# Key-side softmax reciprocals moved from VectorE to ScalarE as exp(-ln), with row normalisations of tiles 2 and 3 freed and a new instruction order

## The chip, the cores and the metric

The kernel runs on one core of a Trainium2 chip. The metric is device microseconds of one execution, lower is better. Kernels are compared only within the same rounds. A difference under 2% counts as the same. All runs used here are fast; the granted TensorE clock of the profiled ones is 1.0 (0.999 in one), that of the timed ones 0.994 to 1.0.

## The reference

```python
x = A_x                                   # 2048 rows x 640
h  = x + A_ref(layernorm(x), wqkv, w_phi, wo)
h2 = h + B_ref(layernorm(h), w_gate, w_up, w_down)

# A_ref: 32 heads of 20 columns
pk    = einsum("bhsd,hdf->bhsf", k, w_phi)                 # pq likewise from q
phi_k = concat([softmax(pk), softmax(-pk)], axis=-1)       # over 20 columns
kv, z = einsum("bhsf,bhsd->bhfd", phi_k, v), sum_s(phi_k)
o     = einsum(phi_q, kv) / (einsum(phi_q, z) + 1e-6)      # then @ wo
# B_ref: ((x @ w_gate) * (x @ w_up)) @ w_down
```

The change touches one step: the two softmaxes of the key side. Per row there are 2 x 32 sums of 20 exponentials each, and the exponentials are multiplied by the reciprocals of the 64 sums.

## The kernel before

The rows are worked in 16 tiles of 128. Each operation has a name and a key; a list scheduler places the operations of every engine in the order of a table of keys, and semaphores follow from the data. So **a table of keys is an order of instructions for TensorE (PE), VectorE, ScalarE, the Pool engine and the queue of transfers (SP)**.

The key side of a tile `t` (bodies cut):

```python
for s in range(2):                                  # exp(+pk), exp(-pk) out of PSUM
    G.op("act",  "Kx%d_%d" % (t, s), ... func=AF.Exp, scale=1.0 - 2.0 * s ...)
G.op("dve",  "Ks%d" % t, ... tensor_reduce(out=SR[.., 0, :], in_=ek, op=ALU.add) ...)
G.op("dve",  "Kr%d" % t, ... reciprocal(out=SR[.., 1, :], in_=SR[.., 0, :]) ...)
G.op("pool", "Kn%d" % t, ... tensor_tensor(out=ek, in0=ek, in1=SR[.., 1, :], op=ALU.mult) ...)
# then KV<t>: the key-value matmuls on PE
```

The rows of a tile are normalised (`xn`), and transposed (`xt`) before the projections. The transposes of tiles 0 to 3 are matmuls on PE. Those of tiles 4 to 15 are transfers in the one SP queue, which also carries later rows of the input, the transposes of the query weights (`wqt0` to `wqt4`), later the transposes of the attention output (`oT`) and the down-projection weights (`wd0` to `wd3`):

```python
TPE = (0, 1, 2, 3)
...
G.op("dve", "xn%d" % t, xn, 0.5, LD, [...], [xb], 10 * t - 22,
     alts=[] if t in TPE else [("act", act_c(640, True), LA)])   # may go to ScalarE
...
else:                                                            # t not in TPE
    G.op("sp", "xt%d" % t, ... dma_start_transpose(out=xnT[tile t], in_=xn) ...)
```

PSUM has 8 banks; three hold the key-value accumulators during the key stage, and a projection needs a pair of what is left.

The softmax here doesn't subtract the row's maximum and nothing guards it: scores larger than these inputs give would overflow.

Of the kernel before, what the change touches and what calls it, by code (L numbers as in the profile page):

```python
# [8 lines left out]
AF = mybir.ActivationFunctionType  # L9
# [30 lines left out]
TPE = (0, 1, 2, 3)  # L40
# [7 lines left out]
x0:0.7 wk0:1.18:1 wk2:1.66:1 wk4:2.14 x1:0.7 wv0:2.14 wv2:2.62:1 wv4:3.1:1 x2:1.66:1 x4:2.62:1 x6:3.58 w5:1.18 x8:4.06 x10:21.175 x12:23.385 x14:19.475  # L48
wqt0:26.485 wqt1:25.265 wqt2:37.415 wqt3:38.635 wqt4:32.535 wo0:51.896 wo2:53.336 wg0:52.856 wu0:51.416 wg1:54.296 wu1:50.936 wg2:49.976 wu2:53.816
wg3:49.016 wu3:52.376 wg4:49.496 wu4:50.456 id0:4.17 gl0:1.52 eps:1.77 id1:4.72 gla0:2.19 glb0:2.63 gla4:2.41 glb4:3.07 gla1:1.97 glb1:3.73 gla2:3.29  # L50
glb2:3.95 gla3:2.85 glb3:3.51 va1:0.7 glx:4.47 kv1:5.12 zero:0.7 warm0:1.08 warm1:1.51 warm2:1.94 warm3:2.37 warm4:2.8 warm5:3.23 warm6:3.66 warm7:4.09
warm8:4.52 warm9:4.74 Ph0:5.42 Ph1:5.2:1 Ph2:5.432:1 WT0:5.27 WTe0:5.819 WT1:5.549 WTe1:6.443:1 WT2:7.062 WTe2:7.612:1 WT3:7.342 WTe3:8.03 WT4:10.677
WTe4:11.226 F1_0:6.747 Fe1_0:7.332:1 F1_1:7.9 Fe1_1:8.485 F1_2:8.215 Fe1_2:9.108:1 F1_3:8.628 Fe1_3:9.732 F1_4:12.143 Fe1_4:12.728:1 L1s0:3.847
L1a0:4.847 L1s1:3.027 L1a1:4.667 L1s2:9.687 L1a2:10.687 L1s3:8.867 L1a3:10.507 L1s4:10.797 L1a4:12.937 L1s5:11.617 L1a5:15.297 L1s6:13.547 L1a6:15.187
L1s7:14.367 L1a7:15.407 L1s8:16.755 L1a8:18.075 L1s9:15.935 L1a9:25.745 L1s10:25.855 L1a10:27.495 L1s11:26.675 L1a11:28.425 L1s12:27.605 L1a12:37.695
L1s13:32.295 L1a13:37.805 L1s14:34.995 L1a14:37.915 L1s15:38.025 L1a15:40.057 L1l0:5.177 L1e0:5.607 L1l1:4.957 L1e1:5.397 L1l2:10.977 L1e2:11.849
L1l4:15.845 L1e4:16.688 L1n4:16.998 L1n5:17.398 L1n6:17.198 L1n7:17.598 L1l8:28.715 L1e8:29.558 L1n8:30.068 L1n9:29.868 L1n10:30.468 L1n11:30.268
L1l12:40.347 L1e12:40.777 L1n12:42.793 L1n13:42.593 L1n14:42.993 L1n15:43.193 xn0:6.288 xt0:7.621 xte0:8.448:1 xn1:5.788 xt1:6.468 xte1:7.018:1
xn2:12.437 xt2:13.833 xte2:14.598 xn3:13.047 xt3:14.112 xte3:15.517:1 xn4:18.035:1 xt4:19.955 xn5:21.241:1 xt5:22.165 xn6:17.575 xt6:18.255 xn7:23.365
xt7:24.045 xn8:31.105:1 xt8:33.755 xn9:30.392:1 xt9:31.315 xn10:33.065:1 xt10:34.975 xn11:35.025:1 xt11:36.195 xn12:43.213:1 xt12:44.136 xn13:44.72  # L60
xt13:46.576 xn14:43.926:1 xt14:45.356 xn15:44.22 xt15:47.796 V0_0:10.133 V0_1:10.405 V0_2:11.871 V0_3:13.001 V0_4:13.273 Ve0:13.975 K0_0:14.391
K0_1:14.663 K0_2:14.935 K0_3:15.206 K0_4:15.478 Kx0_0:16.065 Kx0_1:17.411 Ks0:19.605 Kr0:21.485 Kn0:24.024 KV0:27.975 V1_0:9.59 V1_1:9.862 V1_2:11.6
V1_3:12.458 V1_4:12.73 Ve1:13.351 K1_0:9.047 K1_1:9.318 K1_2:10.956 K1_3:11.227 K1_4:13.561 Kx1_0:15.221 Kx1_1:16.788 Ks1:18.185 Kr1:21.025 Kn1:21.665
KV1:28.651 V2:19.825 Ve2:21.955 K2:15.75 Kx2_0:18.748 Kx2_1:19.995 Ks2:21.945 Kr2:23.865 Kn2:26.383 KV2:32.043 V3:17.108 Ve3:19.371 K3:18.466
Kx3_0:20.618 Kx3_1:22.578 Ks3:24.325 Kr3:29.955 Kn3:30.668 KV3:34.078 V4:23.9 Ve4:25.626 K4:25.258 Kx4_0:26.886 Kx4_1:27.72 Ks4:30.875 Kr4:33.115
Kn4:35.386 KV4:38.829 V5:32.719 Ve5:34.402 K5:26.616 Kx5_0:28.935 Kx5_1:29.768 Ks5:33.575 Kr5:37.235 Kn5:37.875 KV5:42.221 V6:21.183 Ve6:23.201
K6:22.541 Kx6_0:24.17 Kx6_1:25.003 Ks6:28.535 Kr6:30.415 Kn6:33.027 KV6:42.897 V7:29.327 Ve7:31.818 K7:30.685 Kx7_0:32.442 Kx7_1:33.778 Ks7:35.815
Kr7:38.845 Kn7:40.234 KV7:45.247 V8:37.47 Ve8:39.305:1 K8:39.505 Kx8_0:41.133 Kx8_1:41.966 Ks8:42.8 Kr8:45.22 Kn8:45.86 KV8:48.639 V9:34.754 Ve9:36.382
K9:36.112 Kx9_0:37.74 Kx9_1:38.574 Ks9:40.167 Kr9:41.767 Kn9:43.393 KV9:50.674 V10:40.863 Ve10:42.59 K10:43.888 Kx10_0:45.517 Kx10_1:46.35 Ks10:47.183
Kr10:48.783 Kn10:49.423 KV10:54.066 V11:56.101 Ve11:57.73 K11:45.923 Kx11_0:47.551 Kx11_1:48.384 Ks11:49.243 Kr11:52.094 Kn11:52.734 KV11:60.491  # L70
V12:57.46 Ve12:59.088:1 K12:47.281 Kx12_0:49.008 Kx12_1:49.841 Ks12:50.674 Kr12:52.554 Kn12:55.093 KV12:61.167 V13:54.742 Ve13:56.371 K13:51.35
Kx13_0:52.978 Kx13_1:53.811 Ks13:55.243 Kr13:56.843 Kn13:59.811 KV13:62.473 V14:58.818 Ve14:60.446 K14:49.315 Kx14_0:50.944 Kx14_1:51.777 Ks14:53.014
Kr14:54.614 Kn14:57.452 KV14:63.149 V15:64.14 Ve15:65.769 K15:52.708 Kx15_0:54.435 Kx15_1:55.268 Ks15:57.602 Kr15:59.84 Kn15:62.17 KV15:68.736
KVe0:70.902 KVe1:69.682 KVe2:70.292 F0_0:61.843 Fe0_0:62.428 F0_1:60.176 Fe0_1:61.07 F0_2:63.825 Fe0_2:64.41:1 F0_3:43.573 Fe0_3:44.64 F0_4:62.158
Fe0_4:62.743:1 Q0_0:67.657 Qx0_0_0:69.006 Qx0_0_1:69.523 Q0_1:70.491 Qx0_1_0:72.357 Qx0_1_1:71.84 Q0_2:69.412 Qx0_2_0:70.761 Qx0_2_1:71.278 Q0_3:65.499
Qx0_3_0:66.848 Qx0_3_1:67.364 Q0_4:66.578 Qx0_4_0:67.927 Qx0_4_1:68.444 Q1_0:82.274 Qx1_0_0:83.623 Qx1_0_1:84.14 Q1_1:74.419 Qx1_1_0:76.285
Qx1_1_1:75.768 Q1_2:83.353 Qx1_2_0:85.219 Qx1_2_1:84.702 Q1_3:78.691 Qx1_3_0:80.04 Qx1_3_1:80.557 Q1_4:79.77 Qx1_4_0:81.636 Qx1_4_1:81.12 Q2_0:72.995
Qx2_0_0:74.344 Qx2_0_1:74.86 Q2_1:91.421 Qx2_1_0:93.287 Qx2_1_1:92.77 Q2_2:75.498 Qx2_2_0:76.847 Qx2_2_1:77.364 Q2_3:85.79 Qx2_3_0:87.14 Qx2_3_1:87.656
Q2_4:93.859 Qx2_4_0:95.208 Qx2_4_1:95.725 Q3_0:90.342 Qx3_0_0:92.208 Qx3_0_1:91.691 Q3_1:88.228 Qx3_1_0:89.577 Qx3_1_1:90.094 Q3_2:71.57 Qx3_2_0:72.92
Qx3_2_1:73.436 Q3_3:76.577 Qx3_3_0:77.926 Qx3_3_1:78.443 Q3_4:80.85 Qx3_4_0:82.715 Qx3_4_1:82.199 wd0:95.208 wd1:95.688 wd2:99.088 wd3:98.608  # L80
N0_1:72.65 N0_0:74.074 sr0:73.265 rho0:74.689 A0:75.059 B0:76.089 dd0:77.119 rd0:77.509 o0:77.989 oT0:79.41 O0:84.432 h0:86.123 L2s0:87.175 L2a0:88.175
L2v0:88.626 L2r0:89.25 hc0:88.465 hT0:89.996 N1_1:77.656 N1_0:78.346 sr1:78.271 rho1:78.961 A1:79.331 B1:80.361 dd1:81.391 rd1:81.781 o1:82.261:1
oT1:83.173 O1:86.87 h1:88.498 L2s1:89.43 L2a1:90.56 L2v1:90.85 L2r1:92.28 hc1:90.93:1 hT1:91.61 N2_1:89.307 N2_0:89.652 sr2:90.25 rho2:90.74 A2:91.43
B2:92.46 dd2:93.49 rd2:93.88 o2:94.36 oT2:96.168 O2:107.58 h2:109.249 L2s2:110.352 L2a2:111.524 L2v2:111.814 L2r2:112.164 hc2:111.814 hT2:112.737
N3_1:81.929 N3_0:78.001 sr3:82.993 rho3:83.483 A3:83.853 B3:84.883 dd3:85.913 rd3:86.875 o3:87.355 oT3:88.776 O3:92.5 h3:94.18 L2s3:95.111 L2a3:96.241
L2v3:96.531 L2r3:99.163 hc3:96.611:1 hT3:97.388 N4_1:94.938 N4_0:89.997 sr4:95.931 rho4:96.421 A4:97.111 B4:98.313 dd4:99.343 rd4:99.733 o4:100.213
oT4:101.634 O4:111.121 h4:112.75 L2s4:113.811 L2a4:114.821 L2v4:115.111 L2r4:115.851 hc4:115.111 hT4:116.035 N5_1:104.505 N5_0:104.16 sr5:105.295
rho5:105.785 A5:106.155 B5:107.185 dd5:108.387 rd5:108.949 o5:109.429 oT5:110.85 O5:116.775 h5:118.403 L2s5:119.335 L2a5:120.335 L2v5:120.625
L2r5:121.125 hc5:120.625:1 hT5:121.305 N6_1:99.995 N6_0:98.558 sr6:100.61 rho6:101.271 A6:101.641 B6:102.843 dd6:104.045 rd6:104.435 o6:104.915
oT6:106.336 O6:121.393 h6:123.021 L2s6:124.083 L2a6:125.093 L2v6:125.383 L2r6:128.155 hc6:126.805:1 hT6:127.485 N7_1:140.642 N7_0:142.066 sr7:141.257  # L90
rho7:142.681 A7:143.051 B7:144.081 dd7:145.55 rd7:145.94 o7:146.42 oT7:147.841 O7:153.093 h7:154.844 L2s7:155.895 L2a7:157.025 L2v7:157.346
L2r7:158.425 hc7:157.315 hT7:158.716 N8_1:112.48 N8_0:112.825 sr8:113.501 rho8:114.631 A8:115.001 B8:116.031 dd8:117.633 rd8:118.023 o8:118.503
oT8:119.924 O8:123.096 h8:125.203 L2s8:128.285 L2a8:129.315 L2v8:129.605 L2r8:130.295 hc8:129.795:1 hT8:130.475 N9_1:149.165 N9_0:149.51 sr9:149.78
# [113 lines left out]
def act_c(n, ptr=False):  # L207
    return (0.18 if ptr else 0.09) + n / 1200.0
# [10 lines left out]
LD, LA, LP, LT = 0.18, 0.21, 0.15, 0.27  # L219
# [3 lines left out]
def build_graph():  # L223
    G = Graph()
    T = {}
# [255 lines left out]
    for t in range(NT):  # L481
        kk = 10 * t
# [546 lines left out]
```

## Time and profile before

| | before |
|---|---|
| median of 3 runs | 283.46 us (283.19 to 283.81) |
| span of the profiled execution | 280.6 us (that execution timed 282.35 us) |
| PE busy | 275.4 us, 98% |
| waits of PE in all | 2.0 us |
| first transposes that need the second key weights | 7.87 us |
| last matmul ends, span less that | 278.2 us, 2.4 us |

The span is the time between the first and the last record on the core; the timed figure is some 1.75 us longer. The prediction below shows the busy shares, the chain, the waits and the head.

A view that the prediction did not show, and that became the important one, is the SP queue before, from 20 to 28 us (columns: start, length of the issues, engine, line, operation, out<-in, count). The transfers are named by what they move: `xnT<-xn` are transposes of normalised tiles, `scratch<-in_A_wqkv_dram` transposes of query weights, and further below `x_all` input rows.

```profile
22.53 1.20 SPq L458 DMA_TRANSPOSE xnT<-xn  x1
...
25.64 2.66 SPq L300 DMA_TRANSPOSE scratch<-in_A_wqkv_dram  x2
```

The transpose at 22.53 is that of tile 5; a load of rows and the transpose of tile 7 follow, and only then, at 25.64, two query weight transposes. Tile 5 landed at 26.45 us. PE wanted it at 27.35: the unbroken 13.58 us of matmuls from 15.13 that the prediction shows end at 28.71, and the last ten of them (1.36 us) are tile 5's key projection. So it had 0.9 us to spare.

### The profile page before, as it was taken

What the parts mean: (1) busy time and instruction counts of PE and PEld (TensorE: products, weight loads), DVE (VectorE), ACT (ScalarE), POOL (GpSimd) and SP (SyncE); (2) the same over time, 40 slices, a digit from 0 to 9 for tenths busy, and PEclk for the clock granted to TensorE, in tenths of its full rate; (3) what the DMA queues carried; (4) which work ended last, traced back from release to release, by engine and by line L of the source; (5) the groups of instructions that cost most, each with busy time, mean ns of one, the idle gap of its engine ahead of it and who ended that gap; (6) DMA issues with size and microseconds to landing.
All of it is one profiled execution on the core that took longest, in us unless ns stands there. A gap on an engine that the chain in (4) does not pass through costs nothing.

```text
span 280.6 us, 5021 instructions
## 1 busy us (share of the span) xinstructions
PE 275.4 (98%) x2059; PEld 182.7 (65%) x2075; DVE 178.3 (64%) x365; ACT 107.5 (38%) x189; POOL 65.9 (23%) x80
## 2 busy tenths in 40 slices
PE   7999999999999999999999999999999999999996
PEld 2777877776556698774455775455565545588774
DVE  4999996962578888876378964047763273524332
ACT  3798968745886632202133101312313111313100
POOL 6018899792012213022002221002020000000000
PEclk9999999999999999999999999999999999999999
DMA  7719753891011394532102133001211101100001
GB/s 218 255 23 221 85 120 69 262 395 53 0 26 37 61 269 104 72 93 51 22 0 49 36 84 95 0 0 26 48 49 46 47 1 26 23 26 23 26 30 63
DMA packets 43479, 21.98 MB, mean 78 GB/s; under 512 B 34624, under 2 KB 42176, under 8 KB 43456
## 3 DMA queue, kind: packets, MB, share of 16 engines
q1 hardware_dynamic: 42224, 20.19, 30.5%
q10 hardware_dynamic: 1232, 1.47, 1.6%
q8 instruction: 16, 0.26, 0.4%
q14 instruction: 7, 0.06, 0.1%
HBM read 11.00 MB, written 2.62 MB: 49 GB/s over the span
## 4 chain that ended last, share of the span: by engine, by line
PE 96%; DVE 1%; DMA 1%; issue 0%; ACT 0%; DVEq 0%
PE ps L648 37%; PE ps L667 19%; PE ps L471 16%; PE ps L606 8%; PE ps L530 8%; PE ps L563 4%; PE ps L509 4%; PE ps L387 1%; DMA x_all<-in_A_x_dram 1%; PE ps L449 0%; PE ps L368 0%; DVE st L404 0%; DVE Phi L356 0%; DVE st L405 0%; DVE xn L440 0%
## 5 line engine op out<-in xcount | busy, mean ns | idle before, releaser
L648 PE MATMUL ps<-xnT,Wgu 128*128 128x512 bf16 (+1 forms) x588 | 106.4, 336 | 0.6
L648 PEld LDWEIGHTS ps<-xnT,Wgu 128*128 128x128 bf16 x600 | 58.3, 98 | 42.4 <-DVE ev L656 1.2
L653 ACT ACTIVATE scratch<-ps 128x512 bf16<-128x512 f32 (+1 forms) x60 | 30.7, 512 | 104.6 <-PE ps L648 87.5
L667 PE MATMUL ps<-Wp,ev 128*128 128x320 bf16 (+2 forms) x396 | 53.8, 295 | 0.0
L656 DVE TENSOR_TENSOR ev<-ps,scratch 128x512 bf16<-128x512 f32 (+1 forms) x60 | 33.2, 575 | 31.7 <-PE ps L648 16.7
L667 PEld LDWEIGHTS ps<-Wp,ev 128*128 128x128 bf16 x396 | 38.0, 98 | 14.1
L471 PE MATMUL ps<-Wp,xnT 128*128 128x320 bf16 x320 | 45.8, 299 | 0.0
L595 POOL TENSOR_TENSOR scratch<-scratch,sm 128x640 bf16<-128x640 f32 x14 | 17.8, 1273 | 90.9 <-DVE sm L592 90.9
L500 POOL TENSOR_TENSOR ev<-ev,SR 128x1280 bf16<-128x1280 bf16 x16 | 37.3, 2361 | 5.9 <-DVE SR L498 5.9
L471 PEld LDWEIGHTS ps<-Wp,xnT 128*128 128x128 bf16 x320 | 30.7, 98 | 11.3 <-ACT Wp L236 0.2
L679 DVE SCALAR_TENSOR_TENSOR Wp<-ps,rs,x_all 128x640 bf16<-128x640 f32 (+3 forms) x18 | 14.6, 809 | 28.6 <-PE ps L667 28.3
L495 DVE TENSOR_REDUCE SR<-ev 128x64 f32<-128x1280 bf16 x16 | 23.2, 1460 | 2.9 <-ACT ev L492 2.4
L539 ACT ACTIVATE eqT<-ps 128x512 bf16<-128x512 f32 x40 | 21.6, 594 | 7.5 <-PE ps L530 7.5
L606 PE MATMUL ps<-Wo,scratch 128*128 128x320 bf16 x160 | 24.2, 299 | 0.0
L492 ACT ACTIVATE ev<-ps 128x640 bf16<-128x640 f32 x32 | 21.3, 707 | 5.4 <-PE ps L471 4.9
L530 PE MATMUL ps<-xnT,Wp 128*128 128x512 bf16 x96 | 22.8, 379 | 0.2
L610 DVE TENSOR_TENSOR x_all<-ps,x_all 128x640 bf16<-128x640 f32 x16 | 13.1, 820 | 14.4 <-PE ps L606 14.4
L606 PEld LDWEIGHTS ps<-Wo,scratch 128*128 128x128 bf16 x160 | 15.6, 98 | 7.3
L629 ACT ACTIVATE xn<-x_all,mv 128x640 bf16<-128x640 bf16 x10 | 8.3, 827 | 25.7 <-DVE mv L619 25.7
L620 POOL TENSOR_SCALAR ln<-mv 128x1 f32<-128x1 f32 x16 | 3.4, 210 | 62.7 <-DVE mv L619 62.7
L530 PEld LDWEIGHTS ps<-xnT,Wp 128*128 128x128 bf16 x100 | 9.6, 98 | 9.7 <-DVE KVm L516 0.2
L563 PEld LDWEIGHTS ps<-KVm,eqT 128*128 128x128 bf16 x192 | 12.7, 98 | 3.6 <-DVE ev L656 0.2
(58 smaller groups left out, 206.8 us busy)
## 6 DMA issues: line engine op xcount, KB each, us to landing
out_dram<-Wp SPq DMA_DIRECT2D x15, 160.0 KB, 1.8
x_all<-in_A_x_dram SPq DMA_DIRECT2D x6, 320.0 KB, 4.6
Wgu<-in_B_w_gate_dram SPq DMA_DIRECT2D x5, 384.0 KB, 4.6
Wgu<-in_B_w_up_dram SPq DMA_DIRECT2D x5, 384.0 KB, 7.7
Wp<-in_B_w_down_dram SPq DMA_DIRECT2D x4, 480.0 KB, 5.3
scratch<-in_A_wqkv_dram ACTq DMA_DIRECT2D x2, 320.0 KB, 5.5
Wo<-in_A_wo_dram SPq DMA_DIRECT2D x1, 480.0 KB, 9.8
xnT<-xn SPq DMA_TRANSPOSE x28, 2.7
```

Of the source, the lines that this page charges most:

```text
L471: ins = e.matmul(pb(b, hb)[:, 0:320], lhsT=T["xnT"][:, NC - 1 - c, P * t:P * (t + 1)], rhs=T["Wp"][:, kind, c, 320 * hb:320 * (hb + 1)], s ...
L492: G.op("act", "Kx%d_%d" % (t, s), lambda e, s=s, b=b, ek=ek: e.activation(out=T["ek"][:, ek.slots[0], s, :].rearrange("p (b n) -> p b n", ...
L495: G.op("dve", "Ks%d" % t, lambda e, ek=ek, sr=sr: e.tensor_reduce(out=T["SR"][:, sr.slots[0], 0, :], in_=T["ek"][:, ek.slots[0], :, :].rea ...
L500: G.op("pool", "Kn%d" % t, lambda e, ek=ek, sr=sr: e.tensor_tensor(out=T["ek"][:, ek.slots[0], :, :].rearrange("p s (h f) -> p (s h) f", f ...
L530: ins = e.matmul(pb(b)[:, 0:n], lhsT=T["Wp"][:, 0, i, P * c:P * (c + 1)], rhs=T["xnT"][:, NC - 1 - i, o0:o0 + n], start=(i == 0), stop=(i ...
L539: G.op("act", "Qx%d_%d_%d" % (q, c, s), lambda e, s=s, c=c, o0=o0, n=n, b=b: e.activation(out=T["eqT"][:, s, c, o0:o0 + n], in_=pb(b)[:, 0 ...
L563: ins = e.matmul(pb(b, y)[:, 22 * h0:22 * (h0 + j1 - j0)], lhsT=T["eqT"][:, s, c, P * t:P * (t + 1)], rhs=T["KVm"][:, OFF[s, c] + j0:OFF[s ...
L606: ins = e.matmul(pb(b, hb)[:, 0:320], lhsT=T["oT"][:, oT.slots[0], c, :], rhs=T["Wo"][:, c, 320 * hb:320 * (hb + 1)], start=(c == 0), stop ...
L648: ins = e.matmul(pb(b)[:, 0:n], lhsT=T["Wgu"][:, gu, c, P * ft:P * (ft + 1)], rhs=T["xnT"][:, NC - 1 - c, o0:o0 + n], start=(c == 0), stop ...
L653: G.op("act", "g%d_%d" % (bi, ft), lambda e, pg=pg, gt=gt, n=n: e.activation(out=T["gt"][:, gt.slots[0], 0:n], in_=pb(pg)[:, 0:n], func=AF ...
L656: o_ = G.op("dve", "u%d_%d" % (bi, ft), lambda e, pu=pu, gt=gt, hh=hh, ft=ft, n=n: e.tensor_tensor(out=T["hh"][:, hh.slots[0], ft, 0:n], i ...
L667: ins = e.matmul(pb(b, hb)[:, 0:w], lhsT=T["hh"][:, hh.slots[0], ft, P * tt:P * (tt + 1)], rhs=T["Wd"][:, ft, c0 + w * hb:c0 + w * (hb + 1 ...
```

## The change

The intent: VectorE is full at the start of the key stage (4.84 to 5.00 us busy in the windows of 5 us between 15 and 35 us). Its 16 reciprocals go to ScalarE as `1/s = exp(-ln s)`, which is possible because the sums are positive. Normalisations of tiles 2 and 3 may go to ScalarE too, and a new order was searched for the new load.

```diff
-        G.op("dve", "Kr%d" % t, ... e.reciprocal(out=SR[.., 1, :], in_=SR[.., 0, :]), 0.46, LD, ...)
+        G.op("act", "Kr%d" % t, ... e.activation(out=SR[.., 1, :], in_=SR[.., 0, :], func=AF.Ln), 0.24, LA, ...)
+        G.op("act", "Ke%d" % t, ... e.activation(out=SR[.., 1, :], in_=SR[.., 1, :], func=AF.Exp, scale=-1.0), 0.15, LA, ...)
...
-            if t not in TPE:
+            if t > 1:                    # -mean*rstd, which ScalarE's normalisation needs
...
-             alts=[] if t in TPE else [("act", act_c(640, True), LA)])
+             alts=[] if t < 2 else [("act", act_c(640, True), LA)])
```

The whole table of keys is replaced as well. What it does to the two stretches of the SP queue that this document is about:

```
key stage  before: xt6 x14 xt4 x10 xt5 x12 xt7 wqt1 wqt0 xt9 ...
           after:  xt6 xt4 x10 xt7 wqt0 x14 wqt1 xt5 x12 xt8 ...
later      before: wd0 wd1 oT2 hT3 wd3 wd2
           after:  wd3 wd2 wd0 wd1 oT2 hT3
```

## The prediction

> **What bounds the kernel now.** I read the page's busy shares first, then the chain that ended last, then what TensorE (PE) waited for, and last the loads of the other engines by stage.
>
> ```profile
> PE 275.4 (98%) x2059; PEld 182.7 (65%) x2075; DVE 178.3 (64%) x365; ACT 107.5 (38%) x189; POOL 65.9 (23%) x80
> PE 96%; DVE 1%; DMA 1%; issue 0%; ACT 0%; DVEq 0%
> ```
>
> PE is busy for 98% of the span and is 96% of the chain; no other engine is above 64%. A busy PE is not necessarily a PE at full rate, so the second step is the rate. In the chain in order of time:
>
> ```profile
> 15.13 13.58 PE ps L471 x100
> ...
> 245.49 2.73 PE ps L648 x25
> ```
>
> 100 matmuls of 320 columns in 13.58 us are 135.8 ns each, 25 of 256 columns in 2.73 us are 109.2 ns each. That is the full rate (next part), and the granted clock is 1.00 in every stretch I asked for. So PE has no slack inside its busy time. What is left is its idle time:
>
> ```profile
> PE ps L347 <- DVE zero L342: 1.2, 1, 1.2
> PE ps L368 <- DMA scratch<-in_A_wqkv_dram: 0.4, 1, 0.4
> PE ps L449 <- DVE xn L440: 0.2, 1, 0.2
> PE ps L387 <- issue: 0.2, 1, 0.2
> ```
>
> 1.2 + 0.4 + 0.2 + 0.2 = 2.0 us in the whole execution, three of the four before 7 us. The two ends of the span are these:
>
> ```profile
> 6.09 0.73 PE L368 MATMUL ps<-ident,scratch 128*128 128x128 bf16 x10 [0.40 <-DMA scratch<-in_A_wqkv_dram]
> ...
> 271.78 6.40 PE L667 MATMUL ps<-Wp,ev 128*128 128x320 bf16 x53
> ...
> 277.62 1.02 DVE L679 SCALAR_TENSOR_TENSOR Wp<-ps,rs,x_all 128x320 bf16<-128x320 f32 x2 [0.75 <-PE ps L667]
> ```
>
> So the span of 280.6 us is 6.1 us until the first useful matmul (key weights landing), 272.1 us of PE (until 271.78 + 6.40 = 278.18), and 2.4 us of last evictions and last write. The changed operations belong to the key stage, about 15 to 65 us. There VectorE and the Pool engine are full too, without holding PE up (columns: length, then PE, PEld, DVE, ACT, POOL busy with counts, clock, DMA share, GB/s):
>
> ```profile
> 15.00:20.00 5.00, 5.00 (x41) 3.60 (x39) 4.89 (x14) 4.99 (x11) 0.98 (x4) 1.00 0.02 3
> 20.00:25.00 5.00, 5.00 (x39) 3.62 (x37) 5.00 (x8) 4.61 (x8) 3.02 (x2) 1.00 1.01 212
> 30.00:35.00 5.00, 5.00 (x50) 3.86 (x48) 4.84 (x8) 5.00 (x10) 4.67 (x6) 1.00 0.33 66
> ```
>
> The reader is to see three full engines beside a full PE: VectorE is crowded, and relieving it looks attractive, but PE shows no gap that the relief could close.
>
> **What the Trainium skill says.** "TensorE: Matmul & The Clock Gate", Back-to-back issue gap: warm, N/2.4 + 2.5 ns from one matmul to the next, so 135.8 ns for 320 columns and 109.2 for 256. The trace has exactly these. "Perfetto Trace Analysis", Identifying the Most-Contended Engine, warns that matmul busy time is a poor measure of how near PE is to its limit; the spacing settles that here. "ScalarE: Activation LUTs", What ACT_TABLE_LOAD costs: an ACTIVATE with immediate scale and bias takes 186 ns + 0.833 ns per column, each pointer operand adds 93 ns, and neighbours overlap by 93 ns. The trace has 197 ns for a one-column exp, 296 ns for the ln with a bias tensor, and 594 ns for 512 columns (the formula gives 613), so it agrees. The same page, Table sets: ln and exp lie together in one set, one load serves both. The trace has one table load, 1.28 us at 0.78 us, though ln and exp already alternate in the kernel before. The build of the changed kernel has one as well.
>
> **The change part by part.**
>
> Reciprocals off VectorE: 16 of 128x64, 542 ns median, 16 x 0.542 = 8.7 us less VectorE.
>
> Ln and exp on ScalarE: 32 instructions of 64 columns; the skill's formula gives 186 + 53 = 239 ns each, an estimate, so 7.6 us by duration, and 32 x 0.146 = 4.7 us of engine time after the overlap.
>
> Row normalisations: tiles 2 and 3 become free to go to ScalarE, but the new order matters more than the permission. By the listing ScalarE has eight before (tiles 4, 5, 8 to 12, 14) and five after (3, 5, 9, 11, 14). Three at 923 ns leave ScalarE (-2.8 us), three at 593 ns come to VectorE (+1.8 us). Two tiny Pool operations come in (0.4 us). In the later stages three of ScalarE's ten centring passes (827 ns) go to VectorE (about 0.53 us each).
>
> Sum over the span: VectorE 178.3 - 8.7 + 1.8 + 1.6, about 173, plus an attention normalisation that it takes from Pool; ScalarE 107.5 + 7.6 - 2.8 - 2.5, about 110. Neither comes near 280. **All of this lies beside PE, so its direct worth is zero.** PE has the same 299 blocks of matmuls, permuted. What can move the time is whether a wait appears or goes.
>
> Key chain of one tile: from the last key matmul, two exps 1.3 us, row sum 1.43, reciprocal 0.54 with hops, Pool multiply 2.36, then the key-value matmuls. The new pair costs 0.24 + 0.24 and one more hop, and often stands with a 0.6 us exp or copy between its halves: 0 to 0.7 us longer, about 6.5 us in all. In the PE order the work between the end of a tile's key matmuls and its key-value matmuls is 7.8 us at the least before and 8.5 us after. The longer chain still fits.
>
> ScalarE's queue from 14 to 35 us: summed with start-to-start times (0.60 us per exp or copy, 0.81 per normalisation, the pair 0.42), the work up to tile 7's second exp is about 19.2 us before and 18.6 us after, so PSUM is not freed later.
>
> Head: PE waits for the key weights, landing at 6.04 and 7.83 us; these loads keep their places in the queue. Until 7.83 us the same four blocks can run, so the 0.2 us wait for the first normalised tile may go but is swallowed by the second landing: 0. Tile 3's normalisation now follows a weight eviction on ScalarE, whereas PE wants it at about 14.3 us: +0.3 us, estimate.
>
> Query fold: in the kernel before its first block waited briefly at 44.4 us, just after its last transposed weights landed at 44.16. It stands 2.7 us earlier in the new PE order, and the last weight transpose stands two places earlier among transposes of 1.27 us, thus 2.5 us earlier: about 0.
>
> Last feed-forward block: 8.7 us of PE work covered the way from tile 14's output projection to the first matmul that needs it; now 6.5 us do. That way took 6.0 us in the trace (236.84 to 242.83): it just fits, +0.1.
>
> Tail: the last output piece is 192 columns instead of 128, 64 / 0.96 = 67 ns more eviction: +0.1.
>
> Sum: 0 + 0.3 + 0 + 0.1 + 0.1 = +0.5 us at worst count. Against it: waits of 0.2 to 0.4 us that the new order may remove. I halve the difference and take +0.05.
>
> **The rivals.** (1) VectorE was really what spaced PE, and its relief shortens the key stage. For: VectorE at 5.00 of 5 us there. Against: 135.8 ns per matmul and no PE wait. It would have to win 5.7 us to count as faster, and PE idles for 2.0 us in all; at best 282.6. (2) ScalarE, in order, waits for a row sum at each ln and holds up the exps behind it, so PSUM comes free late and PE stalls. For: ScalarE at 4.99 of 5 us at 15 to 20 us, and only three sums in flight. Against: the load sum above. Stalls of 0.2 us at several tiles would give 284.5. (3) The table is reloaded at each ln: 32 x 1.28 = 41 us, 324 us. Against: one load in the build. (4) One warm-up matmul less stands ahead of the first transpose, so the array could run at the slow rate longer; the first ten take 0.43 us each against 0.22 later. Cost at most about 1 us.
>
> **Range and chances.** Before is 283.46 with runs 0.6 us apart; I take 283.5. Below: all PE waits of the head and the query fold gone, 282.7. Above: rival 2 or 4 in part, 284.5. The 2% bounds are 277.8 and 289.1, far outside what any mechanism but rival 3 or a misplaced dependency reaches: faster 0.01, same 0.97, slower 0.02.
>
> **What the new profile would show.** Right: PE still 275 us busy, 98%; VectorE near 173 us, ScalarE near 110 us; ln and exp of 64 columns near 240 ns; one table load; a span of 280 to 281.5. Wrong: PE waits for ScalarE or Pool of over 1 us in the key stage (rival 2), several table loads (rival 3), matmuls spaced below 135 ns per 320 columns or a key stage more than 1 us shorter (rival 1), cold spacing after 6 us (rival 4), or a PE gap just before the last feed-forward block.

## The result, and the profile after

| | before, same job | after |
|---|---|---|
| median of 4 runs | 283.63 us (283.19 to 283.82) | 284.39 us (283.89 to 284.65) |
| ratio | | 1.0027, 95% interval 1.0006 to 1.0048 |
| span of the profiled execution | 280.6 us | 282.4 us |
| PE / VectorE / ScalarE busy | 275.4 / 178.3 / 107.5 us | 275.9 / 175.7 / 108.7 us |

A ratio is the mean time of one kernel's fast runs over that of the other's of the same rounds, so it is not quite the ratio of the medians quoted. The result is the same by the 2% rule, and a little slower: 0.8 us of medians here, and 1.1 us in a repetition on another chip (283.85 against 282.75, ratio 1.0035, 1.0000 to 1.0069). The outputs are right.

The page after, its busy row and the shares of the chain:

```profile
PE 275.9 (98%) x2060; PEld 183.1 (65%) x2075; DVE 175.7 (62%) x355; ACT 108.7 (38%) x215; POOL 65.7 (23%) x82
PE 90%; DMA 7%; SPq 1%; issue 0%; ACTq 0%; ACT 0%; DVE 0%; DVEq 0%
```

The work has moved as intended, and the chain has changed in kind: transfers had 1% of it before and have 7% now. In the waits of PE (total, times, longest):

```profile
...
PE ps L473 <- DMA xnT<-xn: 1.1, 1, 1.1
PE ps L610 <- DMA scratch<-scratch: 0.5, 1, 0.5
...
```

The two of the four that are left out (1.2 and 0.4 us) are of the head and as before. The waits for the first normalised tile and before the query fold (0.2 us each) have gone. Two new ones have come: a projection waits 1.1 us for a transposed tile, and an output projection 0.5 us for a transposed attention output. The chain in order of time leads to the first of them (start, length, what):

```profile
15.23 10.44 PE ps L473 x77
25.68 4.88 DMA xnT<-xn
30.60 1.53 PE ps L473 x10
```

Before, the chain stayed on PE through this time, from 15.13 to 28.71. Here it leaves PE at 25.68 for a transfer that takes 4.88 us, and the tile it brings is tile 5. The timeline of PE (in brackets how long it was idle before, and for what) shows the same from the other side, and the SP queue shows why the transfer started so late:

```profile
30.60 1.53 PE L473 MATMUL ps<-Wp,xnT 128*128 128x320 bf16 x10 [1.10 <-DMA xnT<-xn]
```

```profile
21.29 1.21 SPq L460 DMA_TRANSPOSE xnT<-xn  x1
22.54 1.27 SPq L302 DMA_TRANSPOSE scratch<-in_A_wqkv_dram  x1
23.85 0.58 SPq L274 DMA_DIRECT2D x_all<-in_A_x_dram  x1
24.48 1.16 SPq L302 DMA_TRANSPOSE scratch<-in_A_wqkv_dram  x1
25.68 1.28 SPq L460 DMA_TRANSPOSE xnT<-xn  x1
```

Tile 7's transpose is at 21.29. Then come a query weight transpose, a load of rows and another query weight transpose, and only then, at 25.68, tile 5. Before, its issue stood at 22.53, ahead of both weight transposes. It is issued 3.15 us later and takes 4.9 us instead of 3.9, so it lands 4.1 us later, at 30.55. PE wants it 2.0 us later, at 29.34, when the ten matmuls that began at 27.98 have gone through. Of the 2.1 us between, 0.9 were to spare before; 1.2 us are PE's gap. The loads of the engines for the two windows around the gap (length, then PE, PEld, DVE, ACT, POOL busy with counts, clock, DMA share, GB/s):

```profile
25.00:30.00 5.00, 4.50 (x41) 3.22 (x38) 4.74 (x10) 4.02 (x12) 4.32 (x5) 1.00 1.00 203
30.00:35.00 5.00, 4.40 (x47) 3.57 (x48) 3.94 (x5) 3.68 (x9) 4.11 (x2) 1.00 0.48 97
```

PE has lost 0.50 and 0.60 us of 10, at a full clock; the transfers are at a share of 1.00 in the first window. VectorE, in 30 to 35, has come down from 4.84 to 3.94 us. The relief is there, and PE is no faster for it.

The second new wait, in the queue and on PE:

```profile
95.59 1.97 SPq L274 DMA_DIRECT2D Wp<-in_B_w_down_dram  x4
97.61 1.29 SPq L604 DMA_TRANSPOSE scratch<-scratch  x1
```

```profile
106.46 1.53 PE L610 MATMUL ps<-Wo,scratch 128*128 128x320 bf16 x10 [0.47 <-DMA scratch<-scratch]
```

The transpose of tile 2's attention output is issued behind four loads of the down-projection weights and lands at 106.41, that is 8.8 us after its issue. Before, it stood behind two of them, landed 6.4 us after its issue (97.21 to 103.61), and was wanted only at 108.75.

From these two traces, PE's gaps after minus before are +1.26 (tile 5, gap of 1.3 us in starts of matmuls) + 0.63 (output of tile 2) - 0.3 (query fold) + 0.15 (head), about 1.7 us, and the last matmul starts 1.7 us later (279.64 against 277.96). That is more than the 0.8 to 1.1 us of the medians, because the trace before is of an execution 1.1 us faster than its median, while that of after lies 0.2 us below its own.

### The profile page after: what moved, and what is told of

Read it like the earlier page. It is cut to its first block, busy times and chain, and to the rows that moved or that the text cites. A ratio compares the mean times of both kernels' runs of the same rounds, so it can differ in the third digit from the quotient of the medians.

```text
span 282.4 us, 5039 instructions
## 1 busy us (share of the span) xinstructions
PE 275.9 (98%) x2060; PEld 183.1 (65%) x2075; DVE 175.7 (62%) x355; ACT 108.7 (38%) x215; POOL 65.7 (23%) x82
## 4 chain that ended last, share of the span: by engine, by line
PE 90%; DMA 7%; SPq 1%; issue 0%; ACTq 0%; ACT 0%; DVE 0%; DVEq 0%
PE ps L652 34%; PE ps L671 18%; PE ps L473 14%; PE ps L534 8%; PE ps L610 7%; PE ps L513 4%; PE ps L567 4%; DMA scratch<-scratch 3%; DMA scratch<-in_A_wqkv_dram 2%; DMA xnT<-xn 2%; PE ps L389 1%; SPq L274 1%; PE ps L370 0%; PE ps L451 0%; ACTq L274 0%
## 5 line engine op out<-in xcount | busy, mean ns | idle before, releaser
L473 PE MATMUL ps<-Wp,xnT 128*128 128x320 bf16 x320 | 46.4, 299 | 1.1 <-DMA xnT<-xn 1.1
L599 POOL TENSOR_TENSOR scratch<-scratch,sm 128x640 bf16<-128x640 f32 x13 | 16.5, 1270 | 91.7 <-DVE sm L596 91.4
L567 PE MATMUL ps<-KVm,eqT 128*128 128x154 bf16 (+1 forms) x192 | 15.7, 221 | 0.0
```

What stands on the lines that cost most here:

```text
L473: ins = e.matmul(pb(b, hb)[:, 0:320], lhsT=T["xnT"][:, NC - 1 - c, P * t:P * (t + 1)], rhs=T["Wp"][:, kind, c, 320 * hb:320 * (hb + 1)], s ...
L567: ins = e.matmul(pb(b, y)[:, 22 * h0:22 * (h0 + j1 - j0)], lhsT=T["eqT"][:, s, c, P * t:P * (t + 1)], rhs=T["KVm"][:, OFF[s, c] + j0:OFF[s ...
```

## The experiments

**Theory A:** the slowdown is order in the SP queue, the two transposes named. **Rival B:** it is the operation itself, logarithms on ScalarE that wait for row sums and hold up the exponentials behind them. **Rival C:** it is scatter of the head, with no cause in the change. Twelve runs were made, in three jobs on three chips. To keep the head out, the expectations use the span less the time at which the second key weights land; I read it as the span less the start of the ten PE transposes that need them, which follows within 0.15 us in all traces but two: in before_head the array was slow, and in xn3_dve PE was still at earlier blocks, 0.7 us after the landing.

| run | median us | ratio to before (95%) | span - start = rest |
|---|---|---|---|
| **job 1**, before 282.82 | | | |
| before_again | 282.83 | 0.9992 (0.9954 to 1.0031) | 282.4 - 9.65 = 272.8 |
| xt5_early | 282.70 | 0.9979 (0.9943 to 1.0015) | 280.9 - 8.09 = 272.8 |
| wd_split | 283.79 | 1.0013 (0.9975 to 1.0051) | 282.5 - 8.58 = 273.9 |
| both | 282.67 | 0.9972 (0.9931 to 1.0013) | 281.4 - 8.72 = 272.7 |
| **job 2**, before 282.70 | | | |
| recip_new | 284.75 | 1.0042 (0.9998 to 1.0086) | 282.5 - 7.89 = 274.6 |
| op_old | 284.04 | 1.0032 (0.9977 to 1.0087) | 281.1 - 7.38 = 273.7 |
| ln_long | 283.00 | 0.9984 (0.9939 to 1.0030) | 281.0 - 7.77 = 273.2 |
| head_split | 281.65 | 0.9939 (0.9891 to 0.9987) | 279.8 - 7.05 = 272.8 |
| **job 3**, before 282.75 | | | |
| after_again | 283.85 | 1.0035 (1.0000 to 1.0069) | 281.7 - 7.79 = 273.9 |
| before_head | 282.43 | 0.9972 (0.9937 to 1.0006) | array at half rate, see there |
| xn3_dve | 282.49 | 0.9978 (0.9945 to 1.0012) | 280.5 - 7.62 = 272.9 |
| recip_ln_late | 284.41 | 1.0053 (1.0019 to 1.0086) | 282.3 - 7.76 = 274.5 |

For the two first traces the rest is 280.6 - 7.87 = 272.7 before and 282.4 - 7.86 = 274.5 after.

### The unchanged kernels again: before_again, after_again

Nothing is edited; these show what one execution's trace is worth.

> The kernel before, unchanged, timed against itself and profiled a second time. Its first profile came from an execution of 282.35 us, 1.1 us below its own median of 283.46, while the changed kernel's profile came from a typical one. Theory A (two transfer waits made by the new order of the queue, 1.1 + 0.5 us by the waits view) asks why the timed difference is only 0.76 us: it expects a second profile with a span near 281.5 and PE waits that the first did not show, about 1 us together. Theory B (the first profile is typical and the timing is scattered) expects a span of 280.6 again and a ratio of 1.000 with an interval of about 0.002.

Measured: this execution's span is 282.4 us, as long as the first trace of after, yet the kernel is the one before. The waits of PE:

```profile
PE ps L368 <- DMA scratch<-in_A_wqkv_dram: 2.0, 2, 1.7
...
PE ps L449 <- DVE xn L440: 1.2, 1, 1.2
```

All of the extra time is in the head: the second key weights landed at 9.61 us instead of 7.83, and past that point the execution took 272.8 us against 272.7. So rival C is real as scatter, and a comparison of two spans without taking the head off would have been wrong by 1.8 us here.

> The changed kernel, unchanged, profiled a second time and timed in the same rounds as the other three. Theory A: the wait of 1.1 us for tile 5's transpose is there again, that of tile 2's output projection (0.5 us in the first trace) may be, and the span less the landing of the second key weights is 273.9 to 274.6, so 1.1 to 1.8 us above the kernel before. Rival C (the waits were a chance of one execution): neither wait, 272.8.

Measured on a third chip: the 1.1 us wait for tile 5's transpose again (gap 1.3 us in starts, issue at 25.63, landing at 30.52), no wait for tile 2's output (it landed at 105.56), a rest of 273.9. So the first wait is a property of the kernel and the second appears in some executions only.

### Tile 5's transpose moved forward: xt5_early

```diff
-xt5:24.727
+xt5:21.0
```

Only the SP queue changes; tile 5 now goes right behind tile 7.

> The changed kernel with one transfer moved: the transpose of tile 5's normalised rows is issued right after tile 7's and ahead of a row load and two weight transposes; all other engines keep their order. Theory A: it lands near 25.5 us instead of 30.55, the 1.1 us wait of the key projection of tile 5 is gone, the time falls by 1.0 to 1.3 us to about 283.2. Rival (ScalarE's added ln and exp set the pace of the key stage): PE waits elsewhere in the stage and the time stays within 0.3 us of 284.4.

The SP queue and PE of this run:

```profile
21.53 2.52 SPq L460 DMA_TRANSPOSE xnT<-xn  x2
24.10 1.27 SPq L302 DMA_TRANSPOSE scratch<-in_A_wqkv_dram  x1
```

```profile
28.21 2.88 PE L473 MATMUL ps<-Wp,xnT 128*128 128x320 bf16 x20
30.93 0.85 PE L513 MATMUL ps<-ev 128*128 128x147 bf16 x12
```

Tiles 7 and 5 are issued together, tile 5 lands at 25.79, 3.0 us after its issue at 22.79, and PE runs the 20 matmuls of two projections through in 2.72 us from start to start (28.21 to 30.93), 136 ns each, where after had waited between the two. The rest is 272.8, 1.7 us below after's first trace and 1.1 below its second; the wait for tile 2's output is absent too, but here by luck of the landing (104.84). Theory A holds for its first part: one changed place in a transfer queue gives the time back.

### Tile 2's output ahead of two of the four loads: wd_split

```diff
+    for w_ in ("wd0", "wd1"):
+        G.by[w_].before.append(G.by["oT2"])
```

> The changed kernel with two of the four loads of the down weights held until the transpose of tile 2's attention output is issued, as the order before had it. Theory A: that transpose lands near 103.6 us instead of 106.4, the 0.5 us wait of tile 2's output projection is gone, the time falls by 0.5 to 0.6 us to about 283.8. Rival (the projection stands too early on PE whatever the queue does): the wait stays and the time too.

```profile
96.27 0.91 SPq L274 DMA_DIRECT2D Wp<-in_B_w_down_dram  x2
98.13 1.21 SPq L604 DMA_TRANSPOSE scratch<-scratch  x1
```

The transpose lands at 101.97, 3.8 us after its issue, behind two loads instead of four; the output projection does not wait. The wait for tile 5 is there as it was (1.1 us, landing at 31.23), and the rest is 273.9. That is 0.6 us below after's first trace but equal to its second, in which the wait for tile 2 was absent without any edit; so the 0.5 us is lost in some executions only, and the timing can't show it. In the same rounds it is 1.1 us slower in the median than xt5_early (283.79 against 282.70): the wait for tile 5 was the one that cost.

### Both: both

> Both moves together. Theory A: the two gains add, 1.6 to 1.8 us off, about 282.7, so 0.5 to 1 us faster than the kernel before and no PE wait of over 0.2 us after 8 us. Rival: a third wait takes their place and the time stays above 283.5.

```profile
PE ps L370 <- DMA scratch<-in_A_wqkv_dram: 2.0, 2, 1.4
PE ps L349 <- DVE zero L344: 1.2, 1, 1.2
```

With the two edits together, these are all the waits of PE, and they lie in the head; the rest is 272.7, and the median 282.67 us, next to 282.82 of the kernel before in the same rounds. **This answers where the slowdown came from: all of it was in the order of transfers.** The gain of 0.5 to 1 us over the kernel before that was expected did not come: the ratio is 0.9972, with 1 inside the interval, and the rest is that of the kernel before within 0.1 us. xt5_early alone gives the same time and rest.

### The reciprocals put back on VectorE, all else kept: recip_new

This is `both`, with the order of PE, VectorE, ScalarE, Pool and SP pinned, and one reciprocal right behind each row sum in place of ln and exp. The banks of PSUM were not pinned, which matters below. That pinning itself costs nothing is seen in head_split, which is pinned too and has a rest of 272.8.

```diff
-        G.op("act", "Kr%d" % t, ... func=AF.Ln ...)
-        G.op("act", "Ke%d" % t, ... func=AF.Exp, scale=-1.0 ...)
+        G.op("dve", "Kr%d" % t, ... e.reciprocal(...) ...)
```

> The kernel with both transfer moves, every engine's order pinned, and one part of the change undone: the reciprocals of the key sums are back on VectorE, one instruction right behind each row sum; ln and exp are gone. Measure: the span less the landing of the second key weights, which took out the scatter of the head in six traces (272.7 with both moves, 272.8 twice for the kernel before). Theory A (the operations lie beside PE and only the order of transfers cost time): 272.6 to 272.9 again, no PE wait in the key stage, VectorE 8 us busier. Rival D (the relief of VectorE is worth something and the bad order hid it): a PE wait of 0.3 us or more appears and the measure rises to 273.1 or above.

Measured: a rest of 274.6, which is 1.9 us above `both`, and in the traces this is one wait:

```profile
43.56 0.48 PE L439 MATMUL ps<-Phi,scratch 128*128 128x140 bf16 x6 [1.68 <-ACT ev L544]
```

The query fold waits 1.68 us. The windows of 40 to 45 us, first `both`, then this run:

```profile
40.00:45.00 5.00, 5.00 (x61) 4.16 (x59) 3.71 (x6) 3.24 (x9) 5.00 (x7) 1.00 0.19 38
```

```profile
40.00:45.00 5.00, 3.32 (x40) 2.60 (x39) 4.93 (x11) 2.61 (x5) 4.63 (x7) 1.00 0.42 82
```

VectorE goes from 3.71 to 4.93 us busy in this window, and PE falls from 5.00 to 3.32. So in this order, made for a VectorE without reciprocals, VectorE comes late when they return, and PE waits. The difference of 1.9 us does not contradict the direct worth of zero; it is what the operation costs inside an order that counts on its absence. By timing alone it is not clear of noise (the interval of the ratio begins at 0.9998); recip_ln_late, with the same reciprocals, is (from 1.0019).

### Is it ScalarE's logarithm that blocks there? recip_ln_late

The wait just shown is put down to ScalarE. In its queue an ln of the row statistics of tiles 12 to 15 stood idle for 2.47 us for VectorE, ahead of tile 9's exponentials. I moved it and the exp after it behind them, in the pinned order of ScalarE:

```diff
-Ve8 L1l12 L1e12 Kx9_0 Kx9_1 xn14
+Ve8 Kx9_0 Kx9_1 L1l12 L1e12 xn14
```

> The kernel with the reciprocals back on VectorE in the new order, which lost 2 us in one PE wait of 1.7 us before the first query fold. My reading of its trace: VectorE is late, the ln of tiles 12 to 15 at the head of ScalarE's queue waits for its statistics until 41.7 us and holds the two exps of tile 9, which free PSUM for the fold. Here that ln and its exp stand behind the two exps, nothing else moves. If the reading is right, the wait falls below 0.3 us and the span less the landing of the second key weights returns from 274.7 to 273.2 or less. If VectorE itself is what PE waits for, the wait stays.

```profile
43.40 0.48 PE L439 MATMUL ps<-Phi,scratch 128*128 128x140 bf16 x6 [1.48 <-ACT ev L544]
```

This reading fell. The wait is 1.48 instead of 1.68 us and the time the same within the scatter of the head, so the blocking was worth 0.2 us at most. ScalarE's line in this run shows why:

```profile
41.96 1.30 ACT L544 ACTIVATE ev<-ps 128x640 bf16<-128x640 f32 x2 [2.69 <-PE ps L523]
```

Tile 9's two exponentials now wait for PE's own key matmuls of tile 9, and take 1.3 us. A fold into the pair of banks that they free can't start before 43.26. The kept kernels settle which pair it uses, because the scheduler gives out the banks when the program is built, and it can be run without a chip: in `both` the fold has banks 0 and 1, freed by VectorE's copy of tile 9's values; in recip_new and recip_ln_late it has banks 2 and 3, freed by those exponentials. So recip_new kept the orders, but not this pair. With the other pair it would not have been earlier in this order of VectorE, which in recip_new does the copy only now, until 44.28:

```profile
41.57 1.44 DVE L547 TENSOR_REDUCE SR<-ev 128x64 f32<-128x1280 bf16 x1
43.05 0.55 DVE L550 RECIPROCAL SR<-SR 128x64 f32<-128x64 f32 x1
43.52 0.76 DVE L288 CAST ev<-ps 128x640 bf16<-128x640 f32 x1
```

In `both`, whose head was 0.8 us later, the same copy began at 41.28. So the pair that the fold had there comes free 2 us later here, behind a row sum and a reciprocal. A VectorE order with the copy ahead of that row sum was not run, so how much of the 1.9 us a better order could save stays open.

### The operation put into the old order of PE: op_old

The kernel before, with ln and exp in place of each reciprocal, the exp 0.35 behind the ln in keys. PE and Pool keep their order; two neighbouring pairs in the SP queue swap (`wqt2`, `xt13`). VectorE and ScalarE were not pinned: the scheduler moved some of their operations too (and gave one value projection, `V4`, other PSUM banks).

```diff
-        G.op("dve", "Kr%d" % t, ... e.reciprocal(...) ...)
+        G.op("act", "Kr%d" % t, ... func=AF.Ln ...)
+        G.op("act", "Ke%d" % t, ... func=AF.Exp, scale=-1.0 ...)
```

> The kernel before with the operation change alone: ln and exp on ScalarE in place of the reciprocals; PE's order as before, ScalarE takes the pairs where its own queue has room. Theory A: span less landing of the second key weights 272.6 to 273.0, time within 0.3 us of the kernel before. Rival B (the ln waits for a row sum and holds ScalarE's queue): PE waits for ScalarE in the key stage and 0.5 us or more are lost.

Measured: a rest of 273.7, 1.0 us above before; the timing is wide (282.9 to 286.88, ratio 1.0032 with 1 in its interval). PE has a new wait:

```profile
31.47 1.53 PE L472 MATMUL ps<-Wp,xnT 128*128 128x320 bf16 x10 [0.53 <-ACT ev L493]
```

and a second gap of 0.3 us at 33.5. In ScalarE's queue of this run one sees what stands in front:

```profile
28.24 0.26 ACT L499 ACTIVATE SR<-SR 128x64 f32<-128x64 f32 x1 [0.65 <-DVE SR L496]
28.40 0.69 ACT L493 ACTIVATE ev<-ps 128x640 bf16<-128x640 f32 x1
...
30.56 0.26 ACT L499 ACTIVATE SR<-SR 128x64 f32<-128x64 f32 x1 [0.22 <-DVE SR L496]
```

The lns (L499) stand and wait for VectorE's row sums, 0.65 and 0.22 us, with exponentials (L493) behind them. This is the rival with the in-order ScalarE queue. In after lns wait too (1.5 us in all, five times), but no wait of PE for ScalarE shows there. Why the first row sum is late here is seen on VectorE:

```profile
25.15 0.49 DVE L405 BATCH_NORM_STATS2 st<-x_all 128x6 f32<-128x320 bf16 x1 [1.38 <-DMA x_all<-in_A_x_dram]
```

The scheduler had moved the statistics of tiles 10, 11 and 14 ahead of tile 3's row sum, and those of tile 10 waited 1.38 us for their rows. The row sum began at 26.74; in the kernel before, at 24.53. So the 1.0 us is the price of the operation together with the order of VectorE that came with it. The operation with VectorE's old order kept was not run.

### ScalarE loaded on purpose: ln_long

`both`, with one more ln over 512 columns in front of each ln, written to memory that is not in use then. ScalarE is then busy for 115.0 us, against 108.7 in after: 6.3 us more, where 8.3 were expected.

```diff
-    e.activation(out=SR[.., 1, :], in_=SR[.., 0, :], func=AF.Ln)
+    (e.activation(out=<unused, 512 columns>, in_=SR[.., 0, :] eight times over, func=AF.Ln),
+     e.activation(out=SR[.., 1, :], in_=SR[.., 0, :], func=AF.Ln))[1]
```

> Strain test on the kernel with both transfer moves: ahead of each ln ScalarE does a useless ln over 512 columns, which holds it for some 0.52 us more per tile, 8.3 us in all, with the same results. It measures how much room ScalarE has where the change put work. Theory A: room of about 1 us per tile by the prediction's queue sum, so the measure stays at 272.7 to 273.2. Rival B: ScalarE at 0.9 to 1.0 busy between 15 and 35 us has no room, and the measure rises by 1 to 4 us with PE waits for ScalarE or Pool.

```profile
PE ps L473 <- ACT ev L494: 0.3, 1, 0.3
```

A rest of 273.2, +0.5 us, all of it one gap of 0.5 us in the starts of the matmuls. So ScalarE, as this order loads it, has room for most of as much again before PE feels more than half a microsecond. The timing (283.00, ratio 0.9984) does not tell this apart from `both`.

### The second key weights in two halves: head_split

If PE has no waits but those of the head, the head is what is left. The second key weights come as one load of two 128-row blocks; I split it in two and issued the halves on the two queues (SP and ScalarE's), all other orders pinned as in `both`.

```diff
-    for n_, (a, b_) in enumerate(((0, 2), (2, 4), (4, 5))):      # key weights
+    for n_, (a, b_) in enumerate(((0, 2), (2, 3), (3, 4), (4, 5))):
-SP: w5 x0 x2 wk4 wv2 x6 x8          ScalarE: x1 wk0 wk2 wv0 x4 wv4
+SP: w5 x0 wk2 x2 wk4 wv2 x6 x8      ScalarE: x1 wk0 wk3 wv0 x4 wv4
```

> The kernel with both transfer moves, order pinned, and the second key weights (two row blocks) loaded as two halves on the two queues ahead of the row load of tiles 2 and 3, so that both halves land near 6.5 us instead of 7.8 to 9.6. Theory A says that the head is what still differs from one execution to the next and that its PE wait of 0.4 to 1.9 us is for exactly this load: the wait falls below 0.4 us and the time by 0.4 to 1.0 us, to 282 or less, faster than both kernels. Rival (another load of the head takes its place: the value weights or the row loads come later by as much): the wait moves and the time stays.

```profile
7.05 0.73 PE L421 MATMUL ps<-ident,scratch 128*128 128x128 bf16 x10
```

No wait stands behind that line: the halves landed at 7.00 and 7.22. The only wait of PE left is the 1.2 us at its very start. The median is 281.65 us, **ratio 0.9939 (0.9891 to 0.9987)**, the fastest kernel and the only one whose interval lies wholly below 1. The rest, 272.8, is that of `both`, so what it gains in this trace is the head: 7.05 against 8.72 in `both`, and 7.76 to 8.58 in the other traces of the new order with the unsplit load. The Trainium skill, "DMA: Bandwidth & Descriptors", section Issuing engines are not separate DMA queues, says that transfers started by different engines run on the same 16 DMA engines and interleave, which warns against expecting more bandwidth from the second queue. No run here separates the two queues, so whether splitting the load or moving half of it made the landing earlier is not shown. The kernel was not run in the same rounds as after; against it there are only the ratios to before, 0.9939 here and 1.0027 and 1.0035 there. Nor was it repeated: xn3_dve below, which differs by one normalisation, has 0.9978 with 1 inside its interval, so a gain clear of noise is shown in this job alone.

### The same head on the kernel before: before_head

```diff
-    for n_, (a, b_) in enumerate(((0, 2), (2, 4), (4, 5))):
+    for n_, (a, b_) in enumerate(((0, 2), (2, 3), (3, 4), (4, 5))):
-SP: x0 w5 x2 wk4 wv2 wv4 x6 x8          ScalarE: x1 wk0 wk2 wv0 x4
+SP: x0 w5 wk2 x2 wk4 wv2 wv4 x6 x8      ScalarE: x1 wk0 wk3 wv0 x4
```

> The kernel before with its order pinned and one thing done: the second key weights are loaded as two halves on two queues ahead of the rows of tiles 2 and 3. If the gain of the version with the split head (281.65 us) is the head's alone, this one comes out within 0.3 us of 281.7 and the change proper is worth nothing in either head. If the new order holds a gain of its own, it stays 0.5 us or more behind.

Measured: a median of 282.43, ratio 0.9972 (0.9937 to 1.0006). That is 0.8 us behind 281.65, as the second case of the expectation has it, but 281.65 is of another job and chip; the new order with the same head in this job (xn3_dve, next) is level with it. The profiled execution was its slowest (284.03 us), and shows why it can't be used for the rest:

```profile
6.88 1.25 PE L418 MATMUL ps<-ident,scratch 128*128 128x128 bf16 x10 [1.19 <-DMA scratch<-in_A_wqkv_dram]
```

The first key weights landed at 6.83 us, and ten transposes took 1.25 us where they take 0.73 elsewhere, 107 ns from one to the next instead of 56. The Trainium skill, "TensorE: Matmul & The Clock Gate", section Wait — 56ns, not 53.3ns?, gives 106.7 ns at 128 columns for the cold array and 55.6 for the warm one, and the traces agree with both. So PE ran at half rate until about 10.2 us. In the window from 5 to 10 us the granted clock is given as 1.00 all the same, so that column does not show it; the spacing does.

### Tile 3's normalisation back on VectorE: xn3_dve

`head_split` with tile 3's normalisation on VectorE, right behind that of tile 2.

```diff
-xn3:12.613:1
+xn3:12.613
```

> The version with the split head, in which the one use of the new freedom is undone: the normalisation of tile 3 goes back to VectorE, right behind that of tile 2; the rest of the order stays. The prediction took its move to ScalarE for a loss of 0.3 us at the transpose of tile 3, and the trace after showed none. Theory A: no PE wait in either place, time within 0.2 us of 281.65. Rival: VectorE's 0.55 us more ahead of the key stage lets a row sum come late and costs 0.3 us or more.

Measured: no wait in the key stage, a rest of 272.9 against 272.8. So the permission to go to ScalarE, as this order uses it, is worth nothing that the trace can show. Timed, it was 282.49 here, 0.8 us slower than head_split was in job 2. In this trace the first key weights landed at 5.74 us (5.29 in head_split's) and PE waited 0.5 us more in the head. Whether that is all of the 0.8 us stays open, since head_split did not run again in this job. What the same rounds do show is that before_head and xn3_dve, the two kernels with a split head, are equal at 282.43 and 282.49.

## Why the prediction was right or wrong

The time, 284.39 us, lies inside the range of 282.7 to 284.5, and close to its upper end; the centre of 283.5 was 0.9 us low. The span of 282.4 us lies above the 280 to 281.5 that it named as the sign of being right. By its steps:

- **"All of this lies beside PE, so its direct worth is zero": right.** `both` has the change without its new waits, and a rest of 272.7 us, the same as before. VectorE came to 175.7 us (173 predicted), ScalarE to 108.7 (110), with one table load. The new pair took 256 ns each in the median against the estimated 239.
- **"Three full engines beside a full PE": misread in part.** The lines shown have the Pool engine busy for 0.98, 3.02 and 4.67 us of 5, so at 15 to 25 us only VectorE and ScalarE were near full. Nothing in the sum hangs on it.
- **Head: right.** The second key weights still decide, 7.86 against 7.87 us, and the vanished wait for the first normalised tile gave nothing.
- **Tile 3's normalisation, +0.3 us: wrong, it was 0.** Its PE transposes at 14.51 us ran without a wait, and xn3_dve found nothing to gain.
- **Last feed-forward block, +0.1 us: it was 0**, no wait stands there. **Tail, +0.1 us: right**, 2.5 against 2.4 us.
- **Query fold: true in itself, but here lies the step that failed.** The prediction said that the last weight transpose "stands two places earlier among transposes of 1.27 us, thus 2.5 us earlier: about 0". It did come two places earlier (and landed at 38.61 instead of 44.16, 5.6 us earlier), and the small wait there did vanish. But a place in a queue is taken from something: the step did not ask what the weight transposes were moved ahead of. It was tile 5, landing 4.1 us later for matmuls that moved by only 2 us and with 0.9 us to spare, and the price was a PE wait of 1.1 us, in both traces of after and in wd_split, gone in xt5_early. The same omission missed tile 2's output behind four loads (0.5 us in one of two traces). With the first term in the sum, the estimate would have been 283.5 + 1.1 = 284.6 us, 0.2 above what was measured.
- **The load sum of ScalarE from 14 to 35 us: right in its conclusion**, PSUM was not freed later. But no such sum was made for the SP queue, the one queue that was reordered and not looked at.
- **Rivals.** (1), VectorE as the pacer, did not show: in 30 to 35 us it is busy 0.9 us less and PE is no faster. It has to be put more finely, though, by recip_new: in an order made for a VectorE without them, the reciprocals cost 1.9 us when they come back. (2), the in-order ScalarE, did not make PE wait in after, and did in op_old, for 1.0 us, there together with a changed order of VectorE. (3), the reloaded table, did not happen. (4), the array longer at the slow rate: its first transposes ran cold until about 6.6 us, but behind the landing at 7.8, so it cost nothing in after, though cold spacing after 6 us was named as a sign of being wrong; in before_head it did show.
- **The range was right partly for another reason than it gave.** Its upper end was meant for rivals 2 or 4, and what filled it was the transfer order, which was not among the rivals. That the range held was luck to that extent.

## What to carry to other kernels

Where one engine is saturated, follow every moved operation to the waits it may open on that engine, and do this for the transfer queues as for the engines: a transfer that moves forward pushes others back, and the first question is who needs those, and when. The relief of an engine that is not the bound is worth only what a new order makes of it: here the operation put into the old order of PE cost 1.0 us, taken out of the new order 1.9, each with what the scheduler moved along with it, and both together, transfers mended, nothing. For effects of a microsecond, count from a point behind the scatter of the first loads, and take at least two traces of each kernel.

## What the Trainium skill lacked or had wrong

- "TensorE: Matmul & The Clock Gate", section What's actually happening, gives the warm-up as about 3.4 us of sustained activity, with a transition that varies by 0.5 us. Here the array still ran at half rate at 6.6 us in after, 5.4 us after its first matmul at 1.24 us, with warm-up matmuls spaced 0.43 us and no gap between; in head_split the change came at 5.5 us, and in before_head, after 1.2 us without a matmul, at about 10.2 us. The granted clock of the profile stood at 1.00 all the while in after and before_head; the page's section Seeing it yourself does say that the clock events of a trace are not to be fully trusted.
- "ScalarE: Activation LUTs", section What ACT_TABLE_LOAD costs: its formula gives 239 ns for 64 columns; the trace has a median of 256 ns and 244 to 333 for single ones, so it is 7% low at the median.
- "DMA: Bandwidth & Descriptors": I found no figure there for how long a transposing transfer takes to land when others are under way. Here the shortest were 2.6 us; tile 5's took 3.0 us ahead of two weight transposes and 4.9 behind them; the attention output's took 3.8 us (wd_split) and 6.4 (before) behind two loads of 492 kB (1536 x 640 x 2 bytes in four parts), and 8.0 to 8.8 behind four.
- No page that I read says how much the landing of a first load scatters between executions. The second key weights, in the same place of an unchanged queue, landed at 7.83 us in one execution and at 9.61 us in another; that is more than the whole effect of this change.
